# Attention and mixture of experts on one core: score matmuls with 32 adjacent query columns as the stationary operand and block-diagonal keys

## The chip, the cores and the metric

The kernel runs on one core of one Trainium2 chip. The metric is device time of one execution in microseconds, taken as the median of several runs. The trace is that of one execution, taken by the hardware profiler.

## What is computed

```python
q, k, v: (B=8, H=8, S=576, D=64) float32
stride = 32
scores = q @ k.T / 8
rel = pos[:, None] - pos[None, :]
mask_local   = (rel >= 0) & (rel < 32)                       # heads 0 to 3
mask_strided = (rel >= 0) & (pos_k % 32 == pos_q % 32)       # heads 4 to 7
attn = softmax(where(mask, scores, -1e9))
x = (attn @ v) as rows of tokens                             # (4608, 512)
logits = x @ w_gate + modality_bias[modality_id]             # 8 experts
e = argmax(logits); gate = softmax(logits)[e]
out[token] = gate * (relu(x[token] @ w1[e]) @ w2[e])         # w1 512x1024, w2 1024x512
```

A local query block of 32 looks at its own and the previous block of 32 keys, a band of 64 keys. A strided query looks at the at most 18 keys with its own remainder by 32.

## The kernel before

The work has two stages. **The attention stage** goes over four pairs of batches (`bp`). Each has four local units (one head of two batches, class `Local`) and four strided units (two heads of one batch, class `Strided`), in turn: local, strided, local, and so on, 32 units in all. Below, "pair" is one local unit and the strided one behind it.

A hand-written loop over `n` sets TensorE's order. In step `n` TensorE computes the scores of unit `n`, the transposes (`turn`) of unit `n-2`, the mask matmul (`masks`) of unit `n+1`, which writes the mask into the score bank before the scores are added to it, and the values of unit `n-3`. Then come up to five pieces of work from `extra`: the transposes and routing logits of a finished pair of batches (`finish_pair`, `route`), which hand the tokens to the expert stage. The other engines' orders come from a scheduler; `pin` fixes a few of them.

In a local unit two batches share one matmul. The contraction of 128 rows holds the 64 head dimensions of either batch, interleaved by partition. The tile `qd` holds the queries block-diagonally: the transfers (`load`) write one batch's queries to every second partition and to the columns 0 to 31, the other's to the other partitions and the columns 32 to 63, and the rest stays zero. A score matmul (L338) takes 64 query columns `qd[:, :, i]` as the stationary operand, which lie 18 elements apart, and streams 64 key columns. Its output goes to 64 of the 128 output partitions, in turn to the lower and the upper half; 18 of them make a unit. `masks` prepares two banks of 256 and 320 columns. VectorE takes each bank's row maxima and subtracts them (L345, L346), and ScalarE takes the exponential (L347, L348). `turn` transposes the exponentials in five 128x128 matmuls, ScalarE copies them to `et` (L360, L363), and `values` multiplies with `vv`, the values of the band with a column of ones. `prep` makes the second copy of the values that the band needs: one ScalarE copy (L319) and two VectorE copies (L320, L321).

In a strided unit the score matmul (L424) takes 36 columns of `qz` (two heads, block-diagonal, 32 elements apart) and streams 18 keys; 32 of them make a unit. Behind it stand a softmax of 288 columns, four transposes (`ts`), the spreading to `eb`, 16 matmuls `ot`, and two ScalarE copies to `xc` (L477).

The routing logits in `route` take 32 stationary columns of the gate's weights, adjacent in memory, and stream 256 columns of `xc` (L529), four times for each chunk, or 128 (L534); the output goes to 32 of the output partitions, in turn to four places.

SyncE issues the loads. From step 3 on they are paced: part 0 of unit `n+3` waits for the last values matmul, part 1 for the last score matmul of unit `n`, the two halves of `vv` for the last transpose and the last values matmul. TensorE is kept warm in the start by 13, 4 and 6 matmuls on zeros (`warm`).

**The expert stage** takes slots of 256 tokens of one expert, gathers them by index, and multiplies in three passes with split weights (L926, L940). The first slots hold tokens of the first pairs of batches, so it can start before the last pair is routed.

Of the kernel before, what the change touches and what calls it, by code (L numbers as in the profile page):

```python
# [11 lines left out]
F32 = mybir.dt.float32  # L12
# [55 lines left out]
M_S = M_L + 9 * 64  # L68
# [5 lines left out]
def _place(g, jj):  # L74

    return 16 + jj if g == 8 else 4 * (g // 2) + g % 2 + 2 * jj


def _block(i, bb):

    return (i + 2 * bb) % 18


def _constants():
# [13 lines left out]
    for g in range(9):  # L98
        for jj in range(2):
            for bb in range(2):  # L100
                ok = (kk > qi) & (kk <= qi + STRIDE)
                if _block(_place(g, jj), bb) == 0:
                    ok = ok & (kk >= 32)
                r0 = 64 * jj + 32 * bb
                cb[r0:r0 + 32, M_L + 64 * g:M_L + 64 * g + 64] = np.where(ok, 0, BIG)
    a = np.arange(18)
    causal = np.where(a[None, :] <= a[:, None], 0, BIG)
    for j in range(2):
        for h in range(2):
            r0 = 64 * j + 18 * h  # L110
            cb[r0:r0 + 18, M_S:M_S + 288] = np.tile(causal, (1, 16))
# [6 lines left out]
def _layout(q, k, v, moe_modality_id, moe_w_gate, moe_modality_bias, moe_w1, moe_w2):  # L118
# [4 lines left out]
    def local_t(t):  # L123
        return t[:, :4].reshape(NBP, 2, 4, S, D).transpose(0, 2, 1, 4, 3).reshape(NBP, 4, 2, D, 18, 32)

    qt, kt = local_t(q), local_t(k)
    vr = v[:, :4].reshape(NBP, 2, 4, 18, 32, D).transpose(0, 2, 1, 3, 4, 5)
    qkl = np.zeros((NBP, 4, 2, D, 37, 32), np.float32)
    win = np.zeros((NBP, 4, 2, 32, 18, D + 1), np.float32)
    win[..., D] = 1  # L130
    for bb in range(2):
        for i in range(18):
            blk = _block(i, bb)
            qkl[:, :, bb, :, i] = qt[:, :, bb, :, blk]
            qkl[:, :, bb, :, 19 + i] = kt[:, :, bb, :, blk]
            w = win[:, :, i % 2, :, 2 * (i // 2) + bb] if i < 16 else win[:, :, i - 16, :, 16 + bb]
            w[..., :D] = vr[:, :, bb, blk]
            if blk:
                qkl[:, :, bb, :, 18 + i] = kt[:, :, bb, :, blk - 1]
    ql = np.ascontiguousarray(qkl[:, :, :, :, :18].swapaxes(-1, -2)).reshape(NBP, 4, 2, D, S)  # L140
    kl = qkl[:, :, :, :, 18:].transpose(0, 1, 3, 2, 4, 5).reshape(NBP, 4, P, 19 * 32)
    vl = win.reshape(NBP, 4, 2, 32, 18 * (D + 1))

    def strided_t(t):
        t = t[:, 4:].reshape(B, 2, 2, 18, 32, D).transpose(0, 1, 2, 5, 4, 3)
        return np.ascontiguousarray(t).reshape(B, 2, 2, D, 32, 18)

    vs = v[:, 4:].reshape(B, 2, 2, 18, 4, 2, 4, D).transpose(0, 1, 6, 3, 4, 5, 2, 7)
# [9 lines left out]
    mod = mod.reshape(36, P).transpose(1, 0)  # L158
# [6 lines left out]
        "ql": ql, "kl": kl, "vl": vl, "qs": np.ascontiguousarray(strided_t(q).swapaxes(-1, -2)).reshape(B, 2, 2, D, S),  # L165
        "ks": np.ascontiguousarray(strided_t(k).transpose(0, 1, 3, 2, 4, 5)).reshape(B, 2, P, S), "vs": vs, "w": w,
# [17 lines left out]
def attention_moe(ctx: ExitStack, tc: tile.TileContext, a, out):  # L184
# [56 lines left out]
    def behind(dma, last):  # L241
        return pin(follow(dma, last))
# [43 lines left out]
    qds = zeros(2, [P, 64, 18], "qd")  # L286
    ets = zeros(1, [P, 18, 2, 32], "et")
    qzs = zeros(2, [P, 36, 32], "qz")
    for t in qds + ets:
        nc.vector.memset(t[:], 0.0)  # L290
    for t in qzs:
        nc.gpsimd.memset(t[:], 0.0)


    class Local:
# [5 lines left out]
        def load(self, part, last):  # L301
            if part == 0:
                self.qd = qds[self.n % 2]
                for bb in range(2):
                    behind(nc.sync.dma_start(
                        self.qd[bb::2, 32 * bb:32 * bb + 32, :].rearrange("p q i -> p (q i)"), a["ql"][self.bp, self.h, bb]), last)
            else:
                self.kd = lp.tile([P, 19, 32], F32, tag="kd", name=f"kd{self.n}")
                behind(nc.sync.dma_start(self.kd.rearrange("p i q -> p (i q)"), a["kl"][self.bp, self.h]), last)

        def load_values(self, part, last):
            if part == 0:
                self.vv = lp.tile([P, 18, D + 1], F32, tag="vv", name=f"vv{self.n}")
            r = slice(64 * part + 32, 64 * part + 64)
            behind(nc.sync.dma_start(self.vv[r].rearrange("p i c -> p (i c)"), a["vl"][self.bp, self.h, part]), last)

        def prep(self):
            vv = self.vv
            pin(nc.scalar.copy(vv[64:96], vv[32:64]))  # L319
            pin(nc.vector.tensor_copy(vv[0:32, 2:18, :], vv[96:128, 0:16, :]))  # L320
            pin(nc.vector.tensor_copy(vv[0:32, 0:2, :], vv[96:128, 16:18, :]))  # L321

        def masks(self):
            self.ss = []
            for g0, gn in ((0, 4), (4, 5)):
                s = pa(f"s{self.n}{g0}")[:, :64 * gn]
                nc.tensor.matmul(s, identb, cb[:, M_L + 64 * g0:M_L + 64 * (g0 + gn)], start=True, stop=True)
                self.ss.append((g0, gn, s.rearrange("p (g c) -> p g c", g=gn)))

        def scores(self):  # L330
            n, kd, qd = self.n, self.kd, self.qd
            mx = lp.tile([P, 9], F32, tag="mx", name=f"mx{n}")
            self.ex = ex = lp.tile([P, 11, 64], F32, tag="ex", name=f"ex{n}")
            for g0, gn, s in self.ss:
                for g in range(gn):
                    for jj in range(2):
                        i = _place(g0 + g, jj)
                        at["scores"] = nc.tensor.matmul(  # L338
                            s[64 * jj:64 * jj + 64, g, :],
                            qd[:, :, i],  # L340
                            kd[:, i:2 + i, :].rearrange("p b q -> p (b q)"),
                            start=False, stop=True, skip_group_check=True,
                        )
                m = mx[:, g0:g0 + gn]
                nc.vector.tensor_reduce(m, s, AX.X, ALU.max)  # L345
                nc.vector.tensor_tensor(ex[:, g0:g0 + gn, :], s, m.unsqueeze(2).to_broadcast([P, gn, 64]), ALU.subtract)  # L346
                nc.scalar.activation(ex[:, g0:g0 + 4, :], ex[:, g0:g0 + 4, :], AF.Exp, scale=0.125)  # L347
            nc.scalar.activation(ex[:, 9:11, :], ex[:, 8:9, :].to_broadcast([P, 2, 64]), AF.Exp, scale=0.125)  # L348

        def turn(self):  # L350
            n, ex = self.n, self.ex
            self.et = et = ets[0]
            t1 = pa(f"t1{n}").rearrange("p (g q) -> p g q", g=4)
            for k in range(4):
                turned_to(t1[:, k, :], ex[:, 2 * k:2 * k + 2, :])
            t2 = pa(f"t2{n}")[:, :P]
            turned_to(t2, ex[:, 9:11, :])
            for par in range(2):
                r = slice(64 * par, 64 * par + 64)
                nc.scalar.copy(et[r, 0:16, par, :], t1[r].rearrange("p k (u q) -> p (k u) q", u=4))  # L360
            for jj in range(2):
                r = slice(64 * jj, 64 * jj + 64)
                nc.scalar.copy(et[r, 16:18, jj, :], t2[r, 64 * jj:64 * jj + 64].rearrange("p (b q) -> p b q", b=2))  # L363

        def values(self):
            n, et, vv, xt, h = self.n, self.et, self.vv, self.xt, self.h
            for bb in range(2):
                gn = 5 - bb
                o = pa(f"o{n}{bb}")[:, :(D + 1) * gn].rearrange("p (g c) -> p g c", g=gn)
                for k in range(4):  # L370
                    for jj in range(2):
                        u = 4 * k + 2 * jj + bb
                        at["values"] = nc.tensor.matmul(  # L373
                            o[64 * jj:64 * jj + 64, k, :], et[:, u, :, :].rearrange("p g q -> p (g q)"), vv[:, u, :],
                            start=True, stop=True, skip_group_check=True,
                        )
                if bb == 0:
                    for b2 in range(2):
                        nc.tensor.matmul(
                            o[64 * b2:64 * b2 + 64, 4, :], et[:, 16 + b2, :, :].rearrange("p g q -> p (g q)"),  # L380
                            vv[:, 16 + b2, :], start=True, stop=True, skip_group_check=True,
                        )
                rs = lp.tile([P, 5], F32, tag="rs", name=f"rs{n}{bb}")
# [3 lines left out]
                    xt[:, 5 * bb:5 * bb + gn, D * h:D * h + D], o[:, :, 0:D],  # L387
# [3 lines left out]
    class Strided:  # L391
# [5 lines left out]
        def load(self, part, last):  # L397
            if part == 0:
                self.qz = qzs[self.n % 2]
                for h in range(2):  # L400
                    behind(nc.sync.dma_start(
                        self.qz[h::2, 18 * h:18 * h + 18, :].rearrange("p q r -> p (q r)"), a["qs"][self.b, self.pr, h]), last)
            else:
                self.kz = lp.tile([P, S], F32, tag="kz", name=f"kz{self.n}")
# [746 lines left out]
```

## Time and profile before

| | |
|---|---|
| median of 3 runs | 612.79 us (612.47 to 613.0) |
| the profiled execution | 618.24 us, its span 616.2 us |
| TensorE busy / loading weights | 599.7 / 534.7 us |
| VectorE, ScalarE, GpSimd busy | 441.5, 391.9, 244.1 us |
| the first and last expert matmul of its kind start at | 180.9 and 592.3 us |

The span runs from the first to the last instruction; the execution's own time has some 2 us around it. An fp32 matmul that isn't a transpose appears in the trace as two rows of TensorE, so 18 score matmuls are x36 there. Busy time of overlapping rows is counted once.

### The profile page before, as it was taken

The page shows a single profiled execution, that of the slowest core. Times are in us where ns is not written, and L with a number is a line of the kernel's source. Part 1 is how long each engine was busy: PE and PEld are TensorE (multiplying, and loading weights), DVE is VectorE, ACT ScalarE, POOL GpSimd, SP SyncE. Part 2 cuts the span into 40 slices and gives each one's busy share as a digit, 9 for nine tenths or more (in the row PEclk, how much of TensorE's full clock was granted, in tenths as well). Part 3 has the DMA queues.
Part 4 walks back from the last instruction along what each step waited for, and adds up shares of the span by engine and source line. Part 5 has one row for each costly group of instructions (what it writes and reads, how often), then busy time and mean ns, then how long its engine had stood idle before and what let it go on. Part 6 is the DMA issues. An engine that isn't in the chain of part 4 may idle for free.

```text
span 616.2 us, 15294 instructions
## 1 busy us (share of the span) xinstructions
PE 599.7 (97%) x5997; PEld 534.7 (87%) x5997; DVE 441.5 (72%) x1092; ACT 391.9 (64%) x798; POOL 244.1 (40%) x226
## 2 busy tenths in 40 slices
PE   9999999999889999999999999999999999999995
PEld 5888898897778989999999999999999999999994
DVE  4666685794696979976876876877877777777542
ACT  2666667866687666676656665756666666666652
POOL 1010110024426465465366356456447447433311
PEclk9998999999799999999999999999999999999999
DMA  7975785888745493484393493123223239623521
GB/s 246 237 208 180 234 261 171 275 246 277 237 160 138 154 263 97 133 265 99 111 301 72 131 277 74 42 79 102 37 70 103 50 119 236 136 59 69 201 110 53
DMA packets 69923, 97.25 MB, mean 158 GB/s; under 512 B 48531, under 2 KB 48787, under 8 KB 66260
## 3 DMA queue, kind: packets, MB, share of 16 engines
q0 software_dynamic: 20672, 58.01, 28.0%
q1 hardware_dynamic: 48692, 37.69, 24.7%
q8 instruction: 49, 0.80, 0.5%
q10 hardware_dynamic: 480, 0.51, 0.3%
q14 instruction: 30, 0.25, 0.1%
HBM read 118.66 MB, written 19.18 MB: 224 GB/s over the span
## 4 chain that ended last, share of the span: by engine, by line
PE 90%; ACT 5%; issue 3%; DVE 1%; DMA 0%; POOL 0%; POOLq 0%; ACTq 0%
PE h L926 33%; PE o L940 32%; PE s L338 6%; PE ss L424 4%; PE o L373 3%; PE ot L469 2%; PE t L219 2%; PE xs L219 1%; PE lg L529 1%; PE warm L204 1%; ACT vv L319 1%; PE xl L219 1%; ACT xc L477 1%; PE ts L219 1%; ACT et L360 1%
## 5 line engine op out<-in xcount | busy, mean ns | idle before, releaser
L962 DVE TENSOR_TENSOR wl<-raw,wh 128x512 fp32r<-128x512 f32 x288 | 187.7, 691 | 71.9 <-ACT wh L961 69.8
L961 ACT CAST wh<-raw 128x512 fp32r<-128x512 f32 x288 | 163.9, 619 | 75.2 <-PE o L940 56.2
L926 PE MATMUL h<-xh,wl 128*128 128x256 f32 x576 | 162.7, 283 | 0.0
L926 PE MATMUL h<-xl,wh 128*128 128x256 f32 x576 | 162.6, 283 | 0.0
L926 PE MATMUL h<-xh,wh 128*128 128x256 f32 x576 | 162.4, 282 | 0.1
L808 POOL DMA_INDIRECT raw<-in_w,wi x72 | 87.4, 1215 | 165.6 <-DVE wl L962 125.8
L926 PEld LDWEIGHTS h<-xh,wh 128*128 128x128 f32 x576 | 109.5, 190 | 7.5 <-issue 0.6
L926 PEld LDWEIGHTS h<-xl,wh 128*128 128x128 f32 x576 | 109.6, 190 | 5.5
L940 PE MATMUL o<-wh,hh 128*128 128x512 f32 x288 | 114.2, 396 | 0.0
L940 PE MATMUL o<-wl,hh 128*128 128x512 f32 x288 | 113.8, 395 | 0.0
L926 PEld LDWEIGHTS h<-xh,wl 128*128 128x128 f32 x576 | 109.7, 190 | 1.0
L940 PE MATMUL o<-wh,hl 128*128 128x512 f32 x288 | 110.3, 390 | 0.0
L929 ACT ACTIVATE hh<-h 128x256 fp32r<-128x256 f32 x144 | 55.5, 386 | 61.8 <-PE h L926 52.5
L931 DVE SCALAR_TENSOR_TENSOR hl<-h,hh 128x256 fp32r<-128x256 f32 x144 | 60.6, 421 | 24.7 <-ACT hh L929 21.1
L940 PEld LDWEIGHTS o<-wh,hl 128*128 128x128 f32 x288 | 53.5, 188 | 10.9
L940 PEld LDWEIGHTS o<-wh,hh 128*128 128x128 f32 x288 | 54.6, 189 | 7.6
L940 PEld LDWEIGHTS o<-wl,hh 128*128 128x128 f32 x288 | 54.6, 190 | 5.6
L948 POOL DMA_INDIRECT out<-y,le x36 | 44.4, 1233 | 20.7 <-ACT y L947 11.0
L799 POOL DMA_INDIRECT le<-ld,li x36 | 39.9, 1110 | 12.9 <-issue 10.1
L792 POOL DMA_INDIRECT fx<-xd,le x36 | 39.7, 1103 | 11.0 <-issue 10.7
L484 POOL DMA_DIRECT2D xd<-xt x20 | 14.5, 727 | 68.6 <-ACT xt L493 68.5
L360 ACT COPY et<-t 64x512 f32<-64x512 f32 x32 | 18.6, 580 | 31.6 <-PE t L219 31.2
(191 smaller groups left out, 830.2 us busy)
## 6 DMA issues: line engine op xcount, KB each, us to landing
xd<-xt POOLq DMA_DIRECT2D x16, 512.0 KB
kd<-in_kl SPq DMA_DIRECT2D x16, 304.0 KB
vv<-in_vl SPq DMA_DIRECT2D x32, 146.2 KB
qd<-in_ql SPq DMA_DIRECT2D x32, 144.0 KB
qz<-in_qs SPq DMA_DIRECT2D x32, 144.0 KB
kz<-in_ks SPq DMA_DIRECT2D x16, 288.0 KB
vs<-in_vs SPq DMA_DIRECT2D x16, 288.0 KB
raw<-in_w,wi POOLq DMA_INDIRECT x72
```

The source lines that it names most:

```text
L219: at["turn"] = nc.tensor.transpose(dst, src, ident)
L338: at["scores"] = nc.tensor.matmul(s[64 * jj:64 * jj + 64, g, :], qd[:, :, i], kd[:, i:2 + i, :].rearrange("p b q -> p (b q)"), start=False ...
L792: pin(nc.gpsimd.indirect_dma_start(xt[:, h, :], None, xd[0:xrows, :], IOA(ap=le[:, h, 0:1], axis=0)))
L799: pin(nc.gpsimd.indirect_dma_start(le[:, h, :], None, ld[0:xrows, :], IOA(ap=li[:, s, h:h + 1], axis=0)))
L808: pin(nc.gpsimd.indirect_dma_start(raws[j].rearrange("p f c -> p (f c)"), None, a["w"], IOA(ap=wi[:, s, j:j + 1], axis=0), bounds_check=E ...
L926: nc.tensor.matmul(hp, w[:, a1], x[:, c, :], start=(k == 0), stop=(k == 11))
L929: nc.scalar.activation(hh[:], hp, AF.Relu)
L931: nc.vector.scalar_tensor_tensor(hl[:], hp, 0.0, hh.bitcast(F32), ALU.max, ALU.subtract)
L940: nc.tensor.matmul(os[h], hx[:, m], w[:, 512:1024], start=(f == 0 and i == 0), stop=(f == 7 and i == 2))
L948: outs.add(pin(nc.gpsimd.indirect_dma_start(out, IOA(ap=le[:, h, 0:1], axis=0), y[:], None, bounds_check=NT - 1, oob_is_err=False)))
L961: nc.scalar.copy(wh[:, c], raw[:, c])
L962: nc.vector.tensor_tensor(wl[:, c], raw[:, c], wh[:, c].bitcast(F32), ALU.subtract)
```

## The change

Query and key change places in the block-diagonal form. The queries of a unit are loaded plain (`ql`, `qs`; one transfer of 128 partitions), and the keys are written by two transfers into `kd` and `kz`, tiles that stay zero elsewhere. A local score matmul takes 32 adjacent query columns `q[:, i, :]`, streams 128 columns (64 keys of either batch), and writes to 32 of the output partitions, in turn to four places; there are still 18. A strided one takes 18 adjacent columns and streams 36, also to four places; there are still 32. The masks go to banks of 512 columns and of 128 columns on 64 partitions. Maxima, subtraction and exponential are done for 512 columns at once and for the rest of 128 columns on 64 partitions. The fifth transpose has 64 columns. Blocks stand in their natural order now, so `prep` is one VectorE and one ScalarE copy of 1105 columns, and `vv` is one of two tiles that are zeroed once. Inside a pair of batches the rows of tokens are in another order (two blocks of either batch in turn); the modality index is reordered to match, and the host puts the output's rows back.

```diff
 class Local: load
-                self.qd = qds[self.n % 2]
-                for bb in range(2):
-                    behind(nc.sync.dma_start(
-                        self.qd[bb::2, 32 * bb:32 * bb + 32, :]..., a["ql"][self.bp, self.h, bb]), last)
-            else:
-                self.kd = lp.tile([P, 19, 32], F32, tag="kd", name=f"kd{self.n}")
-                behind(nc.sync.dma_start(self.kd..., a["kl"][self.bp, self.h]), last)
+                self.q = lp.tile([P, 18, 32], F32, tag="ql", name=f"ql{self.n}")
+                behind(nc.sync.dma_start(self.q..., a["ql"][self.bp, self.h]), last)
+            else:
+                self.kd = kds[self.n % 2]
+                for b in range(2):
+                    behind(nc.sync.dma_start(
+                        self.kd[b::2, b, 1:19, :]..., a["kl"][self.bp, self.h, b]), last)
 class Local: prep
-            pin(nc.scalar.copy(vv[64:96], vv[32:64]))
-            pin(nc.vector.tensor_copy(vv[0:32, 2:18, :], vv[96:128, 0:16, :]))
-            pin(nc.vector.tensor_copy(vv[0:32, 0:2, :], vv[96:128, 16:18, :]))
+            pin(nc.vector.tensor_copy(vv[0:32, 1:18, :], vv[32:64, 0:17, :]))
+            pin(nc.scalar.copy(vv[64:96, 1:18, :], vv[96:128, 0:17, :]))
 class Local: scores
-                        at["scores"] = nc.tensor.matmul(
-                            s[64 * jj:64 * jj + 64, g, :],
-                            qd[:, :, i],
-                            kd[:, i:2 + i, :].rearrange("p b q -> p (b q)"),
+                    at["scores"] = nc.tensor.matmul(
+                        s[32 * c:32 * c + 32, 128 * u:128 * u + 128], q[:, i, :], kd[:, :, 32 * i:32 * i + 64],
...
+                nc.vector.tensor_reduce(m, s3, AX.X, ALU.max)
+                nc.vector.tensor_tensor(e3, s3, m..., ALU.subtract)
+                nc.scalar.activation(ex[r, u0:u0 + un, :], ex[r, u0:u0 + un, :], AF.Exp, scale=0.125)
 class Strided: scores
-                        s[64 * j:64 * j + 36, 18 * i:18 * i + 18],
-                        qz[:, :, r],
-                        self.kz[:, 18 * r:18 * r + 18],
+                        sh[32 * c:32 * c + 18, :, 18 * i:18 * i + 18], q[:, r, :], kz[:, :, r, :],
 class Strided: values
-                dst = self.xc[:, base:base + S].rearrange("p (q r) -> p r q", r=32)[:, 16 * g2:16 * g2 + 16, :]
+                dst = self.xc.rearrange("p (i b r) -> p b r i", b=2, r=32)[:, b % 2, 16 * half:16 * half + 16, :]
 kernel
-    return r.results[0]["out_0"]
+    return _tokens(r.results[0]["out_0"])
```

TensorE in a pair without pieces of `finish_pair`, from the local scores (`s`) to the masks of the next local unit; `ss` are the strided scores. Before:

```order
L338 MATMUL s_523<-kd_347,qd_103 64x64 x8
L338 MATMUL s_525<-kd_347,qd_103 64x64 x10
L219 MATMUL t_586<-cf_sb,ex_398 128x128 x4
L219 MATMUL t_591<-cf_sb,ex_398 128x128
L417 LDWEIGHTS cb_sb
L417 MATMUL ss_599<-cb_sb 128x288
L469 MATMUL ot_601<-eb_517,vs_360 64x72 x8
L469 MATMUL ot_611<-eb_517,vs_360 64x72 x8
L424 MATMUL ss_599<-kz_424,qz_106 36x18 x32
L219 MATMUL ts_683<-cf_sb,ens_508 72x128 x4
L327 LDWEIGHTS cb_sb
L327 MATMUL s_694<-cb_sb 128x256
```

The same place of TensorE's order with the change:

```order
L323 MATMUL s_519<-kd_103,ql_302 32x128 x16
L323 MATMUL s_520<-kd_103,ql_302 32x128 x2
L204 MATMUL t_581<-cf_sb,ex_397 128x128 x4
L341 MATMUL t_586<-cf_sb,ex_397 128x64
L392 LDWEIGHTS cb_sb
L392 MATMUL ss_593<-cb_sb 128x288
L441 MATMUL ot_595<-eb_513,vs_359 64x72 x8
L441 MATMUL ot_605<-eb_513,vs_359 64x72 x8
L400 MATMUL ss_593<-kz_105,qs_394 18x2x18 x32
L204 MATMUL ts_676<-cf_sb,ens_504 72x128 x4
L313 LDWEIGHTS cb_sb
L313 MATMUL s_687<-cb_sb 128x512
```

The sequence is the same; the shapes of the score matmuls differ, and the first score bank now takes 16 of the 18.

ScalarE in the same pair, from the copies of `et` to the softmax of the strided unit (`ex` are the local exponentials, `vv` the copy in `prep`). Before:

```order
L360 COPY et_104<-t_586 64x16x32 x2
L347 ACTIVATE ex_558<-ex_558 128x256
L363 COPY et_104<-t_591 64x2x32 x2
L477 COPY xc_120<-ot_601 128x16x18
L347 ACTIVATE ex_558<-ex_558 128x256
L348 ACTIVATE ex_558<-ex_558 128x128
L477 COPY xc_120<-ot_611 128x16x18
L319 COPY vv_437<-vv_437 32x1170
```

The same place with the change, behind a first pair of `et` copies like the one that is shown:

```order
L344 COPY et_106<-t_581 64x16x32
L345 COPY et_106<-t_586 64x2x32
L448 COPY xc_124<-ot_595 128x16x18
L332 ACTIVATE ex_554<-ex_554 128x512
L448 COPY xc_124<-ot_605 128x16x18
L307 COPY vv_107<-vv_107 32x1105
L332 ACTIVATE ex_554<-ex_554 64x128
```

One exponential of 512 columns stands ahead of the `vv` copy in place of three, and the small one stands behind it.

## Rows read from the trace of the kernel before

**Rows 1.** The page: span, and busy time of each engine.
```profile
span 616.2 us, 15294 instructions
PE 599.7 (97%) x5997; PEld 534.7 (87%) x5997; DVE 441.5 (72%) x1092; ACT 391.9 (64%) x798; POOL 244.1 (40%) x226
```

**Rows 2.** Line L926, an expert matmul: durations min/median/max, first and last start.
```profile
L926 PE MATMUL h<-xh,wh x576: 274/283/387, 180.9 to 592.3; 128*128 128x256 f32 x192
```

**Rows 3.** Chain, 0 to 185 us: shares by line, a light pair (start, us).
```profile
by line: PE s L338 18.4%; PE ss L424 12.2%; PE o L373 10.2%; PE ot L469 5.6%; PE t L219 5.2%; PE warm L204 4.2%; ACT vv L319 3.8%; PE xs L219 3.8%; PE xl L219 3.8%; ACT xc L477 3.7%; PE ts L219 3.3%; issue 3.3%; ACT et L360 3.2%; PE lg L529
...
30.70 2.08 PE s L338 x36
...
33.46 0.59 ACT et L360
...
37.20 1.17 ACT vv L319
38.42 0.69 PE o L373 x16
39.22 0.47 PE o L373 x16
39.69 2.11 PE s L338 x36
```

**Rows 4.** The same chain: the start, behind a heavy pair, a heavy pair.
```profile
20.52 0.62 PE o L373 x16
...
65.74 0.70 PE t L219 x5
...
68.51 0.33 PE lt L219 x3
...
71.80 0.62 PE o L373 x16
...
92.91 0.70 PE t L219 x5
...
96.45 2.15 PE ss L424 x64
...
99.41 0.62 PE o L373 x16
...
101.30 1.86 PE lg L529 x32
103.17 0.22 PE lg L534 x8
...
104.85 2.24 PE s L338 x36
```

**Rows 5.** Windows: busy us of each engine, clock, DMA share, GB/s.
```profile
30.00:39.00 9.00, 8.13 (x188) 7.50 (x185) 6.17 (x19) 5.99 (x14) 1.49 (x5) 1.00 0.62 189
...
82.00:91.00 9.00, 9.00 (x201) 8.43 (x200) 7.26 (x24) 5.54 (x12) 2.62 (x4) 1.00 0.90 287
```

**Rows 6.** Timeline of TensorE, 66 to 73 us: start, us, instruction.
```profile
68.35 0.49 PE L219 MATMUL lt<-cf_sb,ls 128*128 128x128 f32 x3
68.77 2.22 PE L424 MATMUL ss<-kz,qz 128*36 128x18 f32 x64
```

**Rows 7.** ScalarE's groups by shape, 20 to 140 us: busy us, mean ns.
```profile
L319 ACT COPY vv<-vv 32x1170 f32<-32x1170 f32 x12 | 14.0, 1165 | 0.3
...
L347 ACT ACTIVATE ex<-ex 128x256 f32<-128x256 f32 x24 | 10.0, 418 | 3.0 <-DVE ex L346 2.7
...
L348 ACT ACTIVATE ex<-ex 128x128 f32<-128x128 f32 x12 | 3.6, 297 | 0.0
```

**Rows 8.** Timeline of SyncE: the first issue of `vv`.
```profile
11.61 0.89 SPq L315 DMA_DIRECT2D vv<-in_vl  x2
```

**Rows 9.** Window, 48 to 51 us: columns as in the other windows.
```profile
48.00:51.00 3.00, 3.00 (x60) 3.00 (x58) 1.90 (x9) 0.59 (x2) 0.00 (x0) 0.51 0.56 179
```

**Rows 10.** Timeline, 39.5 to 50 us: the first values of a pair, and its wait.
```profile
47.40 1.07 PE L373 MATMUL o<-vv,et 128*64 128x65 f32 x16 [0.86 <-ACT vv L319]
```

More of the change, by code (lines that the diff above doesn't have):

```diff
@@ L67 @@
 M_L = M_ID + P
-M_S = M_L + 9 * 64
+M_S = M_L + 10 * 64
 M_TRI = M_S + 16 * 18
@@ L119, in _layout, with local_t, strided_t @@
     q, k, v = (np.asarray(t, np.float32) for t in (q, k, v))
[L123 to L146, printed above, removed]
+    def local_t(t, axes):
+        return np.ascontiguousarray(t[:, :4].reshape(NBP, 2, 4, 18, 32, D).transpose(axes))
+    ql = local_t(q, (0, 2, 5, 1, 3, 4)).reshape(NBP, 4, P, S)
+    kl = local_t(k, (0, 2, 1, 5, 3, 4)).reshape(NBP, 4, 2, D, S)
+    vl = np.ones((NBP, 4, 2, 32, 18, D + 1), np.float32)
+    vl[..., :D] = local_t(v, (0, 2, 1, 4, 3, 5))
+    vl = vl.reshape(NBP, 4, 2, 32, 18 * (D + 1))
+    def strided_t(t, axes):
+        return np.ascontiguousarray(t[:, 4:].reshape(B, 2, 2, 18, 32, D).transpose(axes))
+    qs = strided_t(q, (0, 1, 5, 2, 4, 3)).reshape(B, 2, P, S)
+    ks = strided_t(k, (0, 1, 2, 5, 4, 3)).reshape(B, 2, 2, D, S)
     vs = v[:, 4:].reshape(B, 2, 2, 18, 4, 2, 4, D).transpose(0, 1, 6, 3, 4, 5, 2, 7)
@@ L330, in scores @@
-        def scores(self):
[L331 to L337, printed above, removed]
-                        at["scores"] = nc.tensor.matmul(
-                            s[64 * jj:64 * jj + 64, g, :],
-                            qd[:, :, i],
-                            kd[:, i:2 + i, :].rearrange("p b q -> p (b q)"),
[L342 to L348, printed above, removed]
+            n = self.n
@@ L352, in turn @@
             self.et = et = ets[0]
[L353 to L363, printed above, removed]
+            t1 = pa(f"t1{n}").rearrange("p (u x) -> p u x", u=4)
@@ L365, in values @@
+            for u in range(4):
+                turned_to(t1[:, u, :], ex[:, u, :])
+            t2 = pa(f"t2{n}")[:, 0:64]
+            at["turn"] = nc.tensor.transpose(t2, ex[0:64, 4, :], ident[0:64, 0:64])
+            for b in range(2):
+                r = slice(64 * b, 64 * b + 64)
+                nc.scalar.copy(et[r, 0:16, b, :], t1[r].rearrange("p u (c q) -> p (u c) q", c=4))
+                nc.scalar.copy(et[r, 16:18, b, :], t2[r].rearrange("p (c q) -> p c q", c=2))
         def values(self):
@@ L373, in values @@
                         at["values"] = nc.tensor.matmul(
-                            o[64 * jj:64 * jj + 64, k, :], et[:, u, :, :].rearrange("p g q -> p (g q)"), vv[:, u, :],
+                            o[64 * jj:64 * jj + 64, k, :], et[:, i, :, :].rearrange("p b q -> p (b q)"), vv[:, i, :],
                             start=True, stop=True, skip_group_check=True,
                         )
[L377 to L382, printed above, removed]
```

134 lines of the change are left out of this document (70 added, 64 removed).

## The prediction

> **What bounds the kernel now.** The page comes first [rows 1]: TensorE is busy for 599.7 of the 616.2 us, so a saving on TensorE is worth time unless another engine takes its place. The edit touches only the attention stage, so the next views are the rows of the first expert matmuls, which start at 180.9 us [rows 2], and the chain of waits over 0 to 185 us [rows 3]. Up to there the local scores (L338) hold 18.4% of the chain, about 34 us or 2.1 us for each of the 16 local units, and the strided scores (L424) 12.2%, about 22.6 us, which is 10.5 of 16 strided units at 2.15 us. So local scores are always on the path, and strided scores in some places only.
>
> The chain in order of time shows two kinds of pair (one local and one strided unit). In a **light pair** [rows 3], from 30.70 to 39.69, the chain goes through the local scores (2.08 us) and the transposes, leaves TensorE at 33.46 for ScalarE's copies of `et`, the `xc` copies and the copy of `vv`, and comes back at 38.42 for the values. While ScalarE works (4.9 us), TensorE does `ot`, the strided scores, `ts` and the masks, and then waits. In a **heavy pair** [rows 4], which ends at 104.85, pieces of `finish_pair` fill TensorE and the chain stays on it: 6.5 us from 92.91 to 99.41, with 2.15 us of strided scores. The pair behind a heavy one is like it: 65.74 to 71.80, 6.1 us. I count 16 local score groups: two in the start, three light pairs (21.7, 30.7, 39.7), three heavy, three behind a heavy one, four with VectorE's routing work, and the last.
>
> The other engines set how far a pair can shrink. At 82 to 91 us VectorE is busy for 7.26 of 9 us and the DMA engines 90% [rows 5]; at 30 to 39 us 6.17 us and 62%.
>
> **Local scores.** Every fp32 matmul shows as two rows. The group takes 2.08 us for 36 rows, 58 ns a row [rows 3]. The values (L373) use 64 array columns too and stream 65, yet 16 rows take 0.47 us, 29 ns each; what differs is that their stationary columns are adjacent, and those of the scores lie 18 elements apart. So today the loading of spread columns sets the pace, and the change takes that away. The new instruction has 32 stationary columns, streams 128, and goes in turn to four places of 32 output partitions. This trace has exactly that shape: the routing logits of L534 are 32 columns by 128, written to four places, 8 rows in 0.22 us, 27.5 ns a row, and L529 with 256 streamed columns takes 1.86 us for 32, 58 ns [rows 4], half of which is 29 ns. So 36 rows cost 1.0 to 1.05 us. The last two blocks have only two places to share, which adds about 0.1 us.
>
> A change of array shape also costs: the three transposes of `lt`, which take 0.33 us [rows 4], start at 68.35, and the first strided score row follows at 68.77, 0.09 us later than a fourth would [rows 6]. Between `o` and the local scores there is no such gap now, as both use 64 columns; with 32 there is one. The Trainium skill (TensorEngine Tiling (Array Packing), Key Properties) says that changing the tiling mode drains TensorE; the 0.09 us agrees in kind. New group: 1.2 us, so 0.9 us is saved. If the shape change cost nothing it would be 1.0; if only two places ran side by side, 36 rows at 54 ns give 1.95 us and nothing is saved (a rival below). For the 14 groups behind the start: 14 x 0.9 = **12.6 us**.
>
> **Strided scores.** 64 rows in 2.15 us, 34 ns a row [rows 4]. The new ones have 18 stationary columns, now adjacent, and stream 36. No row has that shape. Below: four rows side by side at the pace of L529 (58 ns a row for 256 columns is 0.23 ns a column), 64 x 36 x 0.23 = 0.5 us. Above: the quickest row of the trace, 27.5 ns, as a floor, 1.76 us. I take 1.1 us, between the two, because nothing is nearer to one of them: saved 1.05 us, where TensorE is the path.
>
> It isn't in the light pairs. There ScalarE's work from `et` to `vv` hides it, and without that cover it would be worth 1.05 us more a pair. In a heavy pair TensorE's 6.5 us become 5.45, just above what ScalarE needs (0.6 us of transposes and 4.7 us, below): 1.05 each. Behind a heavy pair 6.06 us go to about 5.25, 0.8 each. The four pairs with routing work have two whose strided scores are on the path, 0.4 each. Sum 3.15 + 2.4 + 0.8 = **6.4 us**. The shape change before them costs nothing new (the 64-column one had it too).
>
> **ScalarE between `et` and `vv`.** Today it does three exponentials there, two of 256 columns (418 ns) and one of 128 (297 ns), and a copy of `vv` of 1165 ns [rows 7]. After the change one exponential of 512 columns stands ahead of the `vv` copy, and the small one behind it. From 418 and 297 a column costs 0.95 ns, so 512 take about 0.66 us; the `vv` copy loses 65 of 1170 columns, about 0.06 us. The four `et` copies and two `xc` copies stay in number and size. From 4.9 us I expect 4.7 us: 0.2 us in each of six chains that go through ScalarE, **1.2 us**. Bounds: zero, if the wider stride with which `xc` is now written eats it, and 0.46 us each. VectorE's reduction and subtraction of 512 columns in one piece come later than the first 256 did; in the four pairs with routing work VectorE is near full, and I take off 0.2 us each, **-0.8 us**.
>
> **The start.** Two pairs run before 21.7 us. Their four score groups would save 3.9 us, but the first values at 20.52 [rows 4] need `vv`, whose transfers SyncE issues only at 11.61 [rows 8], behind the loads of five units. These must land, and be copied by ScalarE for 1.17 us, before the first `o`. I give the start **2.5 us** (bounds 1 and 3.9).
>
> **What costs nothing.** One transfer of queries and two of keys take the place of two and one: the same number per unit, on the same queue, with the same waits (keys behind the scores, as today), and 16 KB less. The masks go from 576 to 640 columns and the fifth transpose from 128 to 64 columns; these cancel within 0.05 us. The reordered rows change which token stands where inside a pair of batches, not how many tokens an expert has in it, so the expert stage has the same slots. It moves as a whole.
>
> **TensorE's clock.** At 48 to 51 us its granted clock was 0.51, the 1.2 GHz level [rows 9]. It fell behind a wait of 0.86 us for the `vv` copy, and the first 16 rows of the values took 1.07 us [rows 10] instead of 0.69 [rows 3]. TensorE will wait longer in light pairs, so I add one or two such windows at about 1 us: **-1.5 us**.
>
> Sum: 12.6 + 6.4 + 1.2 - 0.8 + 2.5 - 1.5 = 20.4 us. The profiled execution took 618.24 us and its span 616.2; the median of the runs is 612.79, and 20 us off it is **593 us** (the profiled one near 598, the first expert matmul near 161 us).
>
> **Rivals.**
> *A floor under thin rows.* If no row is quicker than 27.5 ns, the strided scores take 1.76 us and the 6.4 us become about 2.4: 597 us. For it: no row of the trace is quicker. Against: rows of L534 do stream 128 columns, and may be held by these. The Trainium skill (TensorEngine Tiling (Array Packing), Instruction Overhead) gives each matmul an overhead of about 60 cycles, so that one column costs what 60 do; by an estimate from that page 64 rows at 2.4 GHz would be 1.6 us, and the time 596 us. The local scores are above this floor either way.
> *VectorE or the transfers take over.* A pair at 82 to 91 us has 7.3 us of VectorE and 8.1 us of DMA [rows 5]. If light and routing pairs cannot go below 8.5 us, nine of them keep about 0.5 us of 1.1 and the heavy ones half of their strided gain: 8 us less, 601 us. Against: at 30 to 39 us the same loads need 62%.
> *All of it counts.* If ScalarE's chain shrinks with the rest, 14 pairs gain 1.95 us and the start 3.9: 31 us, 582 us. Against: 4.9 us of ScalarE's work stay.
> *Only two of the four places run at once.* Then local scores save nothing and strided ones little: about 609 us. Against: L534's pace.
> *Slower: the clock falls in most pairs.* Then the values cost 0.9 us more a pair (36 rows at the pace of 1.07 for 16 instead of 0.69), and the local scores 1.1 more, since streaming would now hold them: 2.0 us a pair. All 14 pairs cold give 28 us against the 21.9 us saved without the clock's term: 619 us. It decides from eleven cold pairs of 14. For it: that wait of 0.86 us will grow to about 1.5. Against: many such waits today without a fall, and the work left streams more densely.
>
> **Numbers.** Chances: forecast 0.52, floor 0.12, VectorE or transfers 0.14, all of it 0.11, only two places 0.05, clock 0.06. The range 583 to 604 holds the first three and the near part of the fourth, about 0.8. A difference under 0.2% (1.2 us) can't be told from none. Faster 0.92, same 0.02, slower 0.06.
>
> **What would show it.** Right: local score groups of about 1.2 us in the chain; strided ones between 0.5 and 1.8 us; light pairs at 7.7 to 8.1 us with the chain through ScalarE's `et`, `xc` and `vv`; heavy ones near 12 us; the first expert matmul near 161 us and the same 435 us behind it. Wrong: score groups still near 2 us; TensorE waiting for key transfers; VectorE's `ex` in the chain of most pairs; a granted clock of 0.5 in more than four windows before the expert stage.

## The result and the profile after

The changed kernel took 597.17 us (median of 4 runs, 593.34 to 599.03) against 612.70 of the kernel before (4 runs, 612.47 to 613.0): a ratio of 0.974, 95% interval 0.968 to 0.980, 15.5 us less. The profiled execution is the quickest of the four, with 593.34 us; that of before had 618.24, above its median. So the two traces lie 24.9 us apart, and the medians 15.5. The runs of the changed kernel spread over 5.7 us where those of before spread over 0.5. The second figure doesn't hold everywhere: in the sets of runs beside the experiments below, the kernel before spread over 2.7 to 3.9 us, and the changed kernel over 6.7. What may widen the spread is taken up there.

The page of the changed kernel, first lines, beside [rows 1]:

```profile
span 591.6 us, 15240 instructions
...
PE 566.6 (96%) x5997; PEld 494.6 (84%) x5997; DVE 437.7 (74%) x1076; ACT 386.1 (65%) x782; POOL 242.0 (41%) x228
```

The first expert matmul, in the changed kernel on L897 (columns as in [rows 2]):

```profile
L897 PE MATMUL h<-xh,wh x576: 274/283/387, 156.5 to 567.9; 128*128 128x256 f32 x192
```

It starts at 156.5 us instead of 180.9, 24.4 us earlier; behind it lie 435.0 us as before (435.3). The whole difference is in the attention stage.

The chain of waits of the changed kernel over 0 to 160 us (start us, us, what): the start, a light pair, the first score group behind a heavy pair and the next, the last heavy pair.

```profile
11.03 5.94 DMA vv<-in_vl
17.07 0.73 DVE vv L306
18.43 1.04 PE ts L204 x4
20.14 1.75 PE o L354 x36
21.90 1.22 PE s L323 x36
...
29.32 1.22 PE s L323 x36
32.64 0.69 ACT xc L448
34.32 1.12 ACT vv L307
35.48 1.26 PE o L354 x34
36.74 1.22 PE s L323 x36
...
121.15 2.26 issue
123.67 0.71 PE ts L204 x4
125.06 1.95 PE o L354 x36
```

A local group takes 1.22 us where it took 2.08 [rows 3]. A light pair, from one score group to the next, takes 7.42 us (29.32 to 36.74) instead of 8.99, and its chain still goes through ScalarE's `xc` and `vv`. The third score group starts at 21.90, no earlier than before (21.71).

TensorE's score groups by shape up to 156 us (busy us, mean ns; idle before them and its cause):

```profile
L323 PE MATMUL s<-kd,ql 128*32 128x128 f32 x504 | 18.3, 276 | 1.2 <-issue 1.2
L400 PE MATMUL ss<-kz,qs 128*18 128x36 f32 x896 | 10.9, 198 | 2.3 <-issue 2.3
```

For the same 14 groups each, the kernel before shows 31.7 and 32.1 us in this view: 13.4 and 21.2 us of TensorE's work are gone. That is 34.6 us, of which 24.4 arrived.

Windows of the changed kernel, columns as in [rows 5]; the second line answers to the later one there, the first and third are its two stretches of low clock:

```profile
18.00:21.00 3.00, 2.57 (x27) 1.89 (x29) 1.77 (x4) 1.41 (x3) 0.00 (x0) 0.52 0.88 249
...
82.00:91.00 9.00, 8.64 (x190) 6.77 (x187) 5.67 (x17) 7.55 (x18) 0.00 (x0) 1.00 0.96 235
...
123.50:127.00 3.50, 3.50 (x51) 2.70 (x51) 2.25 (x10) 1.37 (x4) 0.83 (x1) 0.56 0.91 338
```

Over 60 to 140 us the DMA engines are busy for 0.92 of the time; before it was 0.76.

What TensorE waited for, 20 to 157 us (us in total, times, longest):

```profile
PE o L354 <- ACT vv L307: 3.2, 6, 1.0
PE ts L204 <- DVE ens L419: 3.1, 3, 1.4
PE ss L400 <- issue: 2.3, 1, 2.3
PE en L596 <- POOL hv L590: 1.4, 1, 1.4
PE s L323 <- issue: 1.2, 1, 1.2
```

Keys aren't in it: no score matmul waits for a transfer here. What is new are long waits put down to "issue", for nothing that the profile shows. TensorE's timeline of the longest:

```profile
120.47 0.68 PE L400 MATMUL ss<-kz,qs 128*18 128x36 f32 x56
123.41 0.26 PE L400 MATMUL ss<-kz,qs 128*18 128x36 f32 x8 [2.26 <-issue]
```

It stops inside a group whose operands are all there, and resumes with the same group. The clock falls behind it (0.56, the 1.2 GHz level), and the values take 1.95 us instead of 1.05. This heavy pair lasted 15.97 us; the other two 12.45.

The DMA queues, 120 to 121.2 us (packets, MB, share):

```profile
q8 instruction: 1, 0.02, 6.1%
```

One packet of 16 KB on a queue that carries instructions started there. By its record it took 1.17 us and ended at 121.75, 1.66 us before TensorE went on. The stretch from 121.2 to 123.4 us has none.

### The profile page after: what moved, and what is told of

It is laid out like the page before. It is cut to its first block, busy times and chain, and to the rows that moved or that the text cites. A ratio compares the mean times of both kernels' runs of the same rounds, so it can differ in the third digit from the quotient of the medians.

```text
span 591.6 us, 15240 instructions
## 1 busy us (share of the span) xinstructions
PE 566.6 (96%) x5997; PEld 494.6 (84%) x5997; DVE 437.7 (74%) x1076; ACT 386.1 (65%) x782; POOL 242.0 (41%) x228
## 4 chain that ended last, share of the span: by engine, by line
PE 86%; ACT 4%; issue 3%; DMA 3%; DVE 3%; SPq 1%; POOL 1%; POOLq 0%; ACTq 0%; DVEq 0%
PE h L897 35%; PE o L911 34%; PE o L354 4%; PE s L323 3%; PE ot L441 2%; ACT vv L307 2%; PE lg L500 1%; PE xs L204 1%; DMA vv<-in_vl 1%; PE t L204 1%; ACT xc L448 1%; PE xl L204 1%; PE ts L204 1%; PE en L596 1%; ACT et L344 1%
## 5 line engine op out<-in xcount | busy, mean ns | idle before, releaser
L897 PE MATMUL h<-xh,wl 128*128 128x256 f32 x576 | 162.7, 283 | 0.2 <-DVE wl L933 0.2
L897 PE MATMUL h<-xl,wh 128*128 128x256 f32 x576 | 162.6, 283 | 0.0
L897 PE MATMUL h<-xh,wh 128*128 128x256 f32 x576 | 162.4, 282 | 0.0
L779 POOL DMA_INDIRECT raw<-in_w,wi x72 | 84.5, 1174 | 166.2 <-DVE wl L933 131.9
L897 PEld LDWEIGHTS h<-xh,wh 128*128 128x128 f32 x576 | 109.5, 190 | 7.2 <-issue 0.6
L897 PEld LDWEIGHTS h<-xl,wh 128*128 128x128 f32 x576 | 109.6, 190 | 5.6
L897 PEld LDWEIGHTS h<-xh,wl 128*128 128x128 f32 x576 | 109.7, 190 | 1.4 <-DVE wl L933 0.4
L911 PEld LDWEIGHTS o<-wh,hl 128*128 128x128 f32 x288 | 53.5, 188 | 10.9
L770 POOL DMA_INDIRECT le<-ld,li x36 | 39.6, 1099 | 12.9 <-issue 10.7
```

The costliest lines, as they stand in the source:

```text
L770: pin(nc.gpsimd.indirect_dma_start(le[:, h, :], None, ld[0:xrows, :], IOA(ap=li[:, s, h:h + 1], axis=0)))
L779: pin(nc.gpsimd.indirect_dma_start(raws[j].rearrange("p f c -> p (f c)"), None, a["w"], IOA(ap=wi[:, s, j:j + 1], axis=0), bounds_check=E ...
L897: nc.tensor.matmul(hp, w[:, a1], x[:, c, :], start=(k == 0), stop=(k == 11))
L911: nc.tensor.matmul(os[h], hx[:, m], w[:, 512:1024], start=(f == 0 and i == 0), stop=(f == 7 and i == 2))
```

## Experiments

Two ideas stood against each other. One: the score groups' own durations carry the gain, each part by itself, and a part of it is given back where transfers near their limit delay something. The other: one of the two parts does it all, or VectorE and ScalarE hold what is missing. Every number below is the median of the run named, with the ratio to the kernel before on the same chip.

**The local part alone.** Local units and `prep` as changed, strided units as before.

```diff
 class Strided: scores, against the changed kernel
-                        sh[32 * c:32 * c + 18, :, 18 * i:18 * i + 18], q[:, r, :], kz[:, :, r, :],
+                        s[64 * j:64 * j + 36, 18 * i:18 * i + 18], qz[:, :, r], self.kz[:, 18 * r:18 * r + 18],
```

> The changed kernel with the strided units as they were before (36 spread query columns, 18 streamed keys, 64 output partitions); only the local units are changed. Theory 1 (a pair's path always holds the local scores, and the strided scores only where TensorE and not ScalarE sets the pair): about 0.86 us in each of 14 pairs and ScalarE's shorter chain, so light pairs keep the 7.4 us of the changed kernel, heavy ones go to about 13.2 us, in all 600 to 604 us. Rival (every saved TensorE microsecond counts): local and strided share the gain by their TensorE time, 0.86 to 1.47, so light pairs lose most of theirs and the time is 606 to 608 us.

605.66 us, 0.987 (0.984 to 0.990), 7.6 us less; between the two expectations. In this kernel the strided keys' dimensions are interleaved in another order than the queries', so its strided scores are other numbers; the matmuls have their shapes and number, and behind the first expert matmul lie 435 us as in the changed kernel. Its chain, and TensorE's waits from 20 to 170 us:

```profile
30.18 1.22 PE s L325 x36
...
33.57 1.99 PE ss L401 x64
...
37.83 1.22 PE s L325 x36
```

```profile
PE en L601 <- POOL hv L595: 5.4, 3, 3.2
```

A light pair takes 7.65 us and TensorE never waits for ScalarE in it. The local term is there, but with strided groups of 2 us three pieces of routing wait for GpSimd's `hv`, 5.4 us in all (1.4 in the whole change).

**The strided part alone.**

```diff
 class Strided: scores, against the kernel before
-                        s[64 * j:64 * j + 36, 18 * i:18 * i + 18], qz[:, :, r], self.kz[:, 18 * r:18 * r + 18],
+                        sh[32 * c:32 * c + 18, :, 18 * i:18 * i + 18], q[:, r, :], kz[:, :, r, :],
```

> The kernel before with only the strided units changed (18 adjacent query columns, 36 streamed, four places). Theory 1: strided groups fall to 0.68 us, but the light pairs stay at 9.0 us, since ScalarE's work hides them; heavy pairs and those behind them gain about 0.8 to 1.3 us each, in all 604 to 608 us. Rival (every saved TensorE microsecond counts): 14 x 1.47 = 20 us, 592 us, and light pairs near 7.6 us.

607.89 us, 0.992 (0.990 to 0.995), 5.3 us less, near the 6.4 of the forecast. TensorE's waits, 20 to 171 us:

```profile
PE o L371 <- ACT vv L317: 8.5, 8, 1.7
```

In light pairs the saved time turns into the wait for ScalarE's copy: 1.7 us instead of 0.86 [rows 10]. Even so these pairs shrink to 8.5 us, since the order of ScalarE's small steps shifts; 9.0 was expected. The heavy pairs fell by only 0.2 to 0.5 us and those behind two of them by 0.5, where 0.8 to 1.3 was expected. Both parts are real, and neither carries the whole; 7.6 and 5.3 make 12.9 of 15.5 us.

**Only the columns made adjacent.** The kernel before, its 64 query columns laid next to each other, zeros loaded with them (twice the bytes of these queries).

```diff
-                self.qd = qds[self.n % 2]
...
+                self.qd = lp.tile([P, 18, 64], F32, tag="qd", name=f"qd{self.n}")
+                behind(nc.sync.dma_start(self.qd.rearrange("p i q -> p (i q)"), a["ql"][self.bp, self.h]), last)
...
-                            qd[:, :, i],
+                            qd[:, i, :],
```

> The kernel before with one thing changed in the local units: the block-diagonal queries are stored with the 64 columns of a matmul side by side, and their zeros are loaded from memory too (590 KB a unit in place of 295). Still 64 columns, two places, 64 streamed columns. Theory 2 (spread stationary columns set the pace before): a local group of 36 rows falls from 2.08 to about 1.05 us, as quick as with four places. Rival (it is the four places of 32 columns that make it quick): the group stays near 2 us. The total time also holds the doubled query loads, so it says little here.

One run, 609.47 us beside 613.22. A score group in its chain:

```profile
39.88 1.05 PE s L338 x36
```

2.08 became 1.05 us, 29 ns a row, with the streamed columns and the output places as before. So the spread of the stationary columns alone set the old pace. The other 0.17 us, up to 1.22, come with the rest of the new shape; no run takes that apart. Little of the 16 us that 16 groups saved arrived: the added bytes brought the DMA share to 0.91, and among other waits five put down to "issue", 4.8 us.

**The changed kernel again, and three variants on the same chip.** The changed kernel itself:

> The changed kernel once more, on the same chip as the next three, for its spread: 593 to 599 us in four runs so far, where the kernel before spreads over 0.5 us. Both theories expect a median of 595 to 599 us. Theory 3 (its runs differ by how often TensorE waits for its instruction stream or for transfers): the trace has some such waits again, at other places. Rival (a half-clock window more or less): runs differ by steps of about 1 us only.

597.55 us (595.95 to 602.68, 6 runs), 0.976 (0.973 to 0.980).

First the values of unit 0 loaded ahead of the other loads of the start:

```diff
+            if n == 0:
+                for part in range(2):
+                    units[0].load_values(part, None)
...
-                if 1 <= n <= nu:
+                if n == 2:
```

> The changed kernel with one order of loads altered in the start: the values of the first unit are loaded ahead of the queries and keys of units 3 and 4. Theory 4 (the start gives nothing because the first values are late, which also holds VectorE, in whose order the copy of them stands ahead of the first strided softmax): the values land near 12 us instead of 17, the third local group starts near 19 us instead of 21.8, in all 2 to 3 us less than the changed kernel. Rival (the start is bound by the transfers as a whole): the keys of the third and fourth unit are late instead, and the third group starts within 0.7 us of 21.8.

600.33 us, 0.979 (0.976 to 0.983). The start did what was expected of it, as its chain shows:

```profile
16.79 1.05 PE o L354 x36
17.84 0.88 PE s L323 x25
```

The third score group starts at 17.84 us, 4 us earlier, and the values run at full clock. But the gain is lost behind it. The next pair takes 9.07 us instead of 7.42, because its values wait for the transfer of the next `vv`; and TensorE's waits, 20 to 164 us, put 9.8 us down to "issue" (those over 0.3 us; 3.4 in the changed kernel's first trace), with three stretches of low clock:

```profile
PE ts L204 <- issue: 5.7, 2, 3.2
...
PE o L354 <- DMA vv<-in_vl: 1.7, 1, 1.7
```

Then the changed kernel with few loads: from the third unit of each kind on, queries and keys aren't loaded and those of the first two are used again; the computation of the rest stays.

```diff
+                if self.n >= 2:
+                    self.q = kept["ql", self.n % 2]
+                    return
...
+                if self.n >= 2:
+                    return
```

> The changed kernel without the loads of queries and keys from the third unit of either kind on; later units use the queries and keys of the first ones, so the output is not the reference's. Half of the attention stage's loads are gone. Theory 3 (late transfers and a late instruction stream cost the changed kernel some us a run, and make its runs differ): TensorE's waits put down to nothing that the profile shows, 3.5 us in all, go, the runs agree within 1 us, and the time is 4 to 7 us less than the changed kernel. Rival (ScalarE's chain sets the pairs, and transfers are hidden): at most 1.5 us less, and the same spread.

586.67 us (585.27 to 588.04), 0.957 (0.955 to 0.959): 10.9 us less than the changed kernel. Behind the first expert matmul lie 435 us as before, so the other output doesn't change that stage's time. TensorE's waits, 20 to 149 us, have no "issue" among them, and the clock doesn't fall before the end; the longest:

```profile
PE ts L204 <- DVE ens L431: 4.1, 3, 1.4
PE o L361 <- ACT vv L314: 3.7, 6, 1.0
```

Its chain, a light pair:

```profile
33.22 1.22 PE s L330 x36
...
38.23 1.12 ACT vv L314
...
40.65 1.22 PE s L330 x36
```

7.43 us, as with all loads: transfers don't set a light pair's length. They cost elsewhere, and pair by pair the 8.1 us between the two profiled executions close: 3.5 at the start (third group at 18.4 instead of 21.9), 1.2 in the pair from 99.39 us, 3.6 in the last heavy pair with its "issue" wait and low clock, and nothing else above 0.1. In the pair from 99.39 us the changed kernel's chain names a late `vv`, but it cost nothing: ScalarE's copy started 3.10 us behind the first `et` copy, and 3.08 us with few loads. What the pair lost is the "issue" wait of 1.18 us inside its score group.

Then the copy of `vv` moved from ScalarE to GpSimd (`nc.gpsimd.tensor_copy` for `nc.scalar.copy` on L307):

> The changed kernel with ScalarE's copy of the values (1.1 us a pair, the last step of the chain before the values matmuls) moved to GpSimd. Theory 5 (ScalarE's work between the transposes and the values sets the light pairs): light pairs fall from 7.4 to about 6.5 us, and six to eight pairs give 4 to 7 us. Rival (VectorE or the transfers are just behind ScalarE): pairs fall by 0.3 us or less, and the time is within 1.5 us of the changed kernel.

617.84 us, 1.008 (1.006 to 1.011): slower than the kernel before. Its chain shows why:

```profile
32.30 3.96 DMA rt_sb<-in_rt
...
39.45 1.11 POOL vv L307
...
40.60 1.45 PE o L354 x21
```

The copy itself takes GpSimd the same 1.11 us, but it stands behind routing work that waits for a transfer, and TensorE idled for 5.99 us here and 7.94 us at 166 us.

**The copy of `vv` ahead of ScalarE's `xc` and `ex`.**

```diff
-                nc.scalar.copy(dst, ot.rearrange("p (r q) -> p r q", r=16))
+                pin(nc.scalar.copy(dst, ot.rearrange("p (r q) -> p r q", r=16)))
...
+        if 2 <= n < nu + 2:
+            units[n - 2].prep()
```

(the same call is taken out further down in the step)

> The changed kernel with one order on ScalarE altered: the copy of the values stands right behind the et copies, ahead of the xc copies and the exponential. No work is left out or moved to another engine. Theory 5 (ScalarE's steps between the transposes and the values set the light pairs): 1.9 us of ScalarE's work goes behind the values' start, light pairs fall from 7.4 to about 6.6 us, and the copy leaves the chain ahead of the values; in the time this may be given back through waits for the instruction stream, 592 to 598 us. Rival (VectorE or the transfers are just behind): light pairs stay above 7.2 us.

595.68 us (593.45 to 597.19), 0.969 (0.967 to 0.972), the quickest here that leaves nothing out, 0.7% below the changed kernel by the ratios. A light pair in its chain:

```profile
36.16 1.55 PE s L323 x36
...
41.52 1.05 PE o L354 x36
42.57 1.00 PE s L323 x28
```

6.41 us, although it begins at the low clock. The waits for `vv` are gone, and "issue" waits of 7.5 us have grown.

With the early first values as well:

> The changed kernel with the order of e7_vv_copy_first and the early first values of e4_first_values_early. Theory 5 with theory 3: the third local group starts near 18 us, light pairs are as in e7_vv_copy_first, and TensorE's waits that the profile puts down to nothing grow to 4 us or more, so the median is 592 to 598 us. Rival (the gains add up): 590 us or less.

598.02 us, 0.975 (0.973 to 0.978): again the early start doesn't pay. The third group starts at 17.67 us, but in the pair behind it TensorE waits 2.7 us for the transfer of `vv`; the "issue" waits make 7.7 us.

With the few loads as well (leaving out what the run with few loads leaves out):

> e5_few_loads (queries and keys are loaded for the first two units of either kind only, so the output is not the reference's) with ScalarE's order of e7_vv_copy_first. Theory 5 (ScalarE's order sets light pairs): light pairs near 6.6 us without any wait for the instruction stream, 578 to 582 us against 586.7. Rival (something else holds the pairs at 7.4): within 1.5 us of 586.7.

584.51 us (583.71 to 584.63), 0.952 (0.950 to 0.953): 2.2 us below the run with few loads, or 0.6% by the ratios, less than expected. The three light pairs take 6.09, 7.02 and 6.53 us instead of 7.42, but the later ones stay as they were within 0.3 us, apart from a heavy one that an "issue" wait of 0.98 us made longer, and the stretch behind the last group takes 1.5 us more, part of it at the low clock. The chain of two light pairs says what took over in them:

```profile
33.11 0.73 DVE mx L337 x2
...
35.04 0.74 DVE vv L313
...
35.91 1.23 PE o L361 x34
```

VectorE runs without a gap from 31.67 to 35.78 us, and its own copy of `vv` comes last.

**More loads, in both kernels.** A transfer of 288 KB per pair into a tile that nothing reads.

```diff
+                if self.n >= 3:
+                    more = lp.tile([P, S], F32, tag="more", bufs=3, name=f"more{self.n}")
+                    behind(nc.sync.dma_start(more[:], a["ks"][2 * self.bp + self.h // 2, self.h % 2]), last)
```

(in the changed kernel from `qs`). In the kernel before:

> The kernel before with one more load of 288 KB in each pair from the fourth on, which nobody reads, so that its transfers come per microsecond as close together as the changed kernel's; TensorE's program is untouched. Theory 3 (TensorE's instruction stream is late when the DMA engines are near full): waits of TensorE that the profile puts down to nothing grow from 1.8 to 4 us or more, with a half-clock window or two more, and the runs spread over more than 2 us; 615 to 622 us. Rival (only the denser instruction stream of the changed kernel outruns its supply): at most 2 us of such waits, 612 to 614 us, a spread as before.

613.78 us, 1.000 (0.998 to 1.001): nothing, with a DMA share of 0.87 over 60 to 140 us, and no "issue" wait over 0.3 us. In the changed kernel:

> The changed kernel with one transfer of 288 KB more per pair, into a tile that nothing reads, issued behind the local keys as in the run on the kernel before. There it cost 1.0 us of 612.8, with no wait of TensorE on its own instructions. Theory (transfers close to full delay TensorE's instruction supply, and only the denser stream of the changed kernel outruns it): 604 to 614 us, more or longer waits with no releaser in the profile than the 3.4 us and the one half-clock window behind them in the changed kernel. Rival (these waits come from something else, and the run with few loads won by landing the early loads sooner): within 2 us of 597.5 us. A third outcome is open, that the keys themselves come late: then TensorE waits for key transfers, which would name the queue's share and not the instruction supply.

609.36 us; the kernel before took 619.36 beside it, on a chip that had given 613.86 earlier. No trace shows why, so the ratio counts: 0.983 (0.980 to 0.987), against 0.976 without the loads: 0.7% or 4.4 us more. That puts it near 602 us beside the other runs, just below the 604 that were expected. TensorE's waits, 20 to 171 us:

```profile
PE ss L403 <- issue: 4.5, 9, 0.6
PE s L316 <- issue: 4.4, 1, 4.4
...
PE s L326 <- issue: 2.9, 2, 1.5
```

The sum of those over 0.3 us is 12.2 us instead of 3.4, and no score matmul waits for keys. What slowed the kernel before at that time may have a part in them. In the changed kernel loads cost time, in the steps few, as they are, more: 586.7, 597.5, some 602 us.

## Why the prediction was right, step by step

The time, 597.17, lay in the range and 4.2 us above the forecast. Terms behind it were off in both directions.

**Local scores: right.** 1.2 us expected, 1.22 measured, 0.86 a group. The reason was right too: adjacent columns alone give 29 ns a row.

**Strided scores: saved more.** 1.1 us was taken, between 0.5 and 1.76. The chain of the variant with `vv` first shows `39.89 0.68 PE ss L400 x58`: 11.7 ns a row, some 0.75 us for 64. The rival of a floor at 27.5 ns a row is refuted. Its other form, an estimate of 25 ns a row from the 60 cycles that the Trainium skill (TensorEngine Tiling (Array Packing), Instruction Overhead) gives each matmul, is refuted as the prediction counted it; but a matmul of the program leaves two rows, 23.4 ns together, close to that figure, and no run here settles which of the two counts is meant. My lower bound, 0.23 ns a column with four rows side by side, was the nearer one. The heavy pairs gained 1.66 us nevertheless (14.11 to 12.45), not 1.95: with TensorE's part shorter, the chain there goes through ScalarE from 46.05 to 51.06 us, and the values wait 0.36 us for an `xc` copy of `finish_pair`.

**ScalarE's chain: mis-sized.** From the last transpose to the values it took 5.04 us and takes 4.35: 0.69 less, where 0.2 was counted. The groups by shape, to set beside [rows 7]:

```profile
L307 ACT COPY vv<-vv 32x1105 f32<-32x1105 f32 x13 | 14.4, 1110 | 0.3
L332 ACT ACTIVATE ex<-ex 128x512 f32<-128x512 f32 x13 | 8.2, 634 | 0.1
```

Each single duration came out as estimated (0.63 us for 0.66, and 0.06 off the copy). But in the chain the exponentials went from 0.83 to 0.43 us, near the bound of 0.46, and the small `et` copies, which I took as unchanged, from 0.42 to 0.23. Light pairs became 7.42 us, below the 7.7 to 8.1 that were expected.

**VectorE: right in kind, too small.** It was to cost 0.8 us; three waits of the transposes for `ens` make 3.1 us, where the kernel before had one of 0.7.

**The start: wrong.** 2.5 us expected, none came. The step that failed is that only the first `o` hangs on the late `vv`. VectorE's own copy of `vv` stands ahead of `ens` in its order (before, `ens` came first, at 15.90 us, and the copy at 17.41), so the transposes `ts` waited as well, for 3.04 us; then the clock was at 0.52, and the values took 1.75 us. The run with early values shows that the 4 us were to be had there.

**The clock: right in number, twice the cost, by another way.** Two stretches of 3.4 us in the first trace, three in the second, behind idle times of 1.5 to 3 us, not behind the 0.55 to 1.02 us waits of light pairs. In the first trace each made the rows in it some 1.5 us longer (in the later one `ts` took 0.71 us instead of 0.56, the masks 0.67 instead of 0.39, the values 1.95 instead of 1.05), so the term of 1.5 us is 3.0. The slower rival, low clock in most pairs, is seen in no trace.

**What the sum didn't have.** Without disturbance, in the run with few loads, the gain is 26 us: 20.8 in the thirteen pairs from the third group on (18.5 counted; three pairs of before that held low clock or "issue" waits are taken at the length of their like), 3.3 at the start, 2.2 behind the last group. Of this the transfers take 10.9 us back, which the rival on transfers had in size (8 us) but not in place: light pairs kept their length, and TensorE waited for no keys. It lost time in its start and in waits without a releaser, with low clock behind them. That 597 came out near 593 is thus partly luck: the pairs and the last stretch gained more than was counted, and the loads took more back.

## What to carry to other kernels

Lay stationary columns next to each other before anything else is changed: the same matmuls ran at half the duration. When TensorE's work shrinks, the same bytes have to move in less time: look at the load on the DMA engines as a whole, not only at the transfers that TensorE waits for. Here the loads of queries and keys cost 11 us, though behind the start no score matmul waited for one. An early start was worth nothing in its two runs, since waits for the next values and waits without a releaser followed it.

## What the hardware showed unexpectedly

**TensorE stands still behind packets of instructions when the DMA engines are busy.** It stops, mostly inside a group, with nothing to wait for that the profile shows, and goes on 1.3 to 1.7 us after the end of a 16 KB packet on the instruction queue q8. By the packets' records that held for all 24 such waits of over 1 us, in eight traces, with packets some 6 us apart. Every trace has 25 of these packets ahead of the expert stage, most without such a wait behind them, and they take 1.1 to 1.2 us on average with few loads as with many; if they are the cause, the delay lies ahead of a packet. The waits' sum against the DMA share over 60 to 140 us:

| kernel | DMA share | "issue" waits over 0.3 us, from 20 us to the expert stage |
|---|---|---|
| few loads; with `vv` first | 0.55; 0.54 | 0; 1.0 us |
| before | 0.76 | 1.3 us, all under 0.5 each |
| `vv` copy on GpSimd | 0.82 | 3.7 us |
| strided alone; local alone; before with more loads | 0.85; 0.86; 0.87 | 0; 0; 0 |
| early values; `vv` first; both | 0.87; 0.89; 0.90 | 9.8; 7.5; 7.7 us |
| changed with more loads | 0.90 | 12.2 us |
| 64 adjacent columns; changed; changed again | 0.91; 0.92; 0.92 | 4.8; 3.4; 5.9 us |

Taking loads away took the waits away, all but one; but from 0.82 to 0.92 the sums don't follow the share. Of the 12.2 us with more loads, 3.5 are seven waits of about 0.5 us, one every 0.75 us at 144 to 146 and 155 to 156 us, which don't follow the packets; the kernel before has three like them, and their cause is open. That the packet causes the longer waits is read from times, not shown by an experiment on the queue. Whether the denser stream of instructions adds to the share is open: before with more loads had 0.87 and no wait, early values had 0.87 and 9.8 us, but 64 adjacent columns, nearly as slow a stream as before, had 0.91 and 4.8 us. These waits fall differently in each trace, which fits the wider spread: 6.7 us in six runs of the changed kernel, 2.8 and 0.9 with few loads.

**Thin matmuls in four places** ran at 11.7 ns a row, 18 stationary and 36 streamed columns, less than half of the 27.5 ns of the quickest rows of before [rows 4].
